# Four VectorE sums of a weight placed between the links of a routing chain, and a flag's transpose given another PSUM bank

## The chip, the cores and the metric

The kernel runs on one core of one Trainium2 chip. The metric is the device time of one execution in microseconds (us). Engines are named as in the profile: PE is TensorE's matmul and PEld its weight load, DVE is VectorE, ACT is ScalarE, POOL is GpSimd, and SP is SyncE, which here only issues transfers.

## What is computed

The reference is a causal attention with a window of 64 positions (8 batches, 8 heads, 576 positions, head size 64), whose output of 4608 rows by 512 is fed to a mixture of 8 experts. Each row goes to exactly one expert, and the choice depends on the row before it:

```python
fresh_e = int(np.argmax(logits[b, s]))
if s == 0 or local_gate[b, s] < 0.5:
    e = fresh_e
else:
    e = prev_e if prev_e >= 0 else fresh_e
prev_e = e
...
h = np.maximum(x[b, s] @ w1[e], 0.0)
out[b, s] = p[e] * (h @ w2[e])
```

So the expert of a row is either its own best expert or that of the row before. All is in float32; W1 is 512 by 1024 and W2 1024 by 512 for each expert.

## The kernel before

**Stages.** Attention runs first, for the first 135 us of the profiled execution or so. It writes its rows to a tensor in HBM (`xs`), the last of these writes from a tile `x` at 134.1 us. Then come blocks of rows, one expert each: two tiles of 128 rows are gathered from `xs`, turned on PE, multiplied by W1, put through a relu, multiplied by W2, scaled, and scattered to the output. Routing decides which rows make up a block. It is done in two parts: the rows of the first three of eight batches are routed during attention, which is enough to fill three blocks (numbered -1, -2 and -3), and all other rows are routed (`second`) while the blocks -1 and -2 run.

**The chain of routing.** `Router.gate` finds the expert of each row by scans on DVE over chunks of 128 rows, then over the chunks. Each step goes to PE to be transposed and back to DVE. In the profile's lines: DVE makes `vk`; PE turns it (L809); DVE copies it and scans twice (`loc` L814, `thru` L815); PE turns the last columns (L819, L820); DVE copies them and scans over the chunks (`crow` L822, `carry` L825); PE turns that (L829); DVE copies it and finishes the rows (`cbs` L831, `ex` L833); PE turns `ex` (L841); DVE copies it and compares (`et` L843, `oh` L845, a memset on `oh` L847); PE sums over rows (L853, L854); DVE copies the sums (L856), and some eighty small DVE instructions follow, which end in the tables `lo` and `hi` (L923, L924), and after the one-hot tables and the matmuls on them (L975), in the indices of the gathers.

PE's order is written out by hand: between two of the chain's transposes stand some matmuls of block -1's product with W1 (`hidden`, L1402). [...]

**The blocks' products.** The product with W2 (`big_result`, all matmuls at L1309) is done with seven products of half-size instead of eight. It needs four sums of quarters of W2, here called t1 to t4 (`right`, L1222, one DVE instruction of 128x1024 each, written to the tile `ws2`, shown as `ws`), and four sums of quarters of `h`, here called s1 to s4 (`halves`/`left`, L1214, 128x512 each, shown as `hs`). On PE the seven products stand in this order: one without sums, s1 with t1, s2 with t2, one without sums, s3 with t3, s4 with a quarter of W2, and a quarter of `h` with t4. (The code's lists count from zero: t1 is `t[0]`.) ACT copies some results out of PSUM (`keep`, L1314), and DVE combines others with what was kept (`put`, L1318, written to `y`). The last product adds on top of a bank from which the second `put` has read, and so waits for it.

**What sets the order on DVE.** In these stages a scheduler places DVE's instructions. A mark given to `issue_after` keeps an instruction behind the marked one. Before the change all four sums of W2, and the four of `h`, of block -1 stand behind `rt.link`, the memset at the end of the chain (L847); those of block -2 stand behind the making of `hi`. For block -1 that is done in `hidden`:

```python
if link and m == link[0]:
    mark = link[1]().ins
    with self.tc.issue_after(mark):
        self.prepare2(st)
```

**The flag.** `flag` turns a column on PE (L161) and reduces it on DVE, to tell whether a slow, rare path has to be taken. It stands after the last matmuls on the tables (L975), and `psum()` is routing's only bank, `r`, from which DVE copies the table (`t`, L977). A second pool, `ps_y` with two banks, is used only by blocks of fewer rows, which come later. Block -3's first stage stands behind the flag's last instruction.

**Transfers.** SP loads weights into a ring of four buffers, each load waiting for the buffer's last reader. POOL issues the gathers and the scatters, one after the other on its queue; a scatter waits until the one before it has landed.

Of the kernel before, what the change touches and what calls it, by code (L numbers as in the profile page):

```python
# [8 lines left out]
F32 = mybir.dt.float32  # L9
# [4 lines left out]
Alu = mybir.AluOpType  # L14
# [5 lines left out]
P = 128  # L20
B, H, S, DH = 8, 8, 576, 64
D = H * DH
E, F = 8, 1024
DK, FK = D // P, F // P
# [674 lines left out]
class Router:  # L699
# [9 lines left out]
    def __init__(self, ctx, tc, lt, xs, tabs, ident):  # L709
        self.nc, self.lt, self.xs, self.tabs, self.ident = tc.nc, lt, xs, tabs, ident  # L710
        self.pool = ctx.enter_context(tc.tile_pool(name="rt", bufs=1))
        self.tc, self.behind = tc, None
        self.rows_of(ctx, tc, "rt_oh1")

    def rows_of(self, ctx, tc, name, bufs=2):
# [47 lines left out]
    @staticmethod  # L763
    def last(ap):
        return ap.rearrange("p (c o) -> p c o", o=1)
# [5 lines left out]
    def gate(self, part, psum):  # L771
# [40 lines left out]
        loc = tl("loc", CMAX, P)[:n]  # L812
        thru = tl("thru", CMAX, P)[:n]
        vec.tensor_tensor_scan(loc, ts[:, 1, :], ts[:, 0, :], 0.0, Alu.mult, Alu.add)  # L814
        vec.tensor_tensor_scan(thru, ts[:, 1, :], self.zero[:n, :P], 1.0, Alu.mult, Alu.add)  # L815
        yield 1.5, True

        cps = psum()[:1, :2 * n].rearrange("o (i c) -> o i c", i=2)
# [3 lines left out]
        vec.tensor_copy(crow, cps)  # L822
        carry = tl("carry", 1, CMAX + 1)[:, :n + 1]
        vec.memset(carry[:, 0:1], 0.0)
        vec.tensor_tensor_scan(carry[:, 1:], crow[:, 1, :], crow[:, 0, :], 0.0, Alu.mult, Alu.add)  # L825
        yield 0.8, True

        cb = psum()[:n, :1]
# [1 line left out]
        cbs = tl("cbs", CMAX, 1)[:n]  # L830
        vec.tensor_copy(cbs, cb)  # L831
        ex = tl("ex", CMAX, P)[:n]
        vec.scalar_tensor_tensor(ex, thru, cbs, loc, Alu.mult, Alu.add)  # L833
        sm = by_chunk("sm")
        vec.tensor_reduce(sm, pa, axis=AX.X, op=Alu.add)
        vec.tensor_scalar(sm, sm, 1e-9, None, Alu.add)
# [7 lines left out]
        oh = self.oh[:, cs]  # L844
        vec.tensor_tensor(oh, last(et).to_broadcast(CE), self.io8.to_broadcast(CE), op=Alu.is_equal)  # L845

        self.link = vec.memset(oh[:CUT, 0, :] if part else oh[CUT:, n - 1, :], 0.0)  # L847
        yield 0.6, True


# [53 lines left out]
    def places(self, pl, n):  # L904

        vec = self.nc.vector

        def tl(name, p, n, dt=F32):
            return self.tl(name, p, CV, dt=dt)[:, :n]

        plc = tl("plc", P, n)
        vec.tensor_reduce(plc, pl, axis=AX.X, op=Alu.add)

        vec.memset(plc[CUT:, C1 - 1:C1], float(2 * N))
        if n > C1:
            vec.memset(plc[:CUT, C1:C1 + 1], float(2 * N))
        plc_i = tl("plc_i", P, n, dt=I32)
        vec.tensor_copy(plc_i, plc)
        lo_i = tl("lo_i", P, n, dt=I32)
        vec.tensor_scalar(lo_i, plc_i, P - 1, None, Alu.bitwise_and)  # L920
        vec.tensor_scalar(plc_i, plc_i, P.bit_length() - 1, None, Alu.arith_shift_right)
        lo, hi = tl("lo", P, n), tl("hi", P, n)
        vec.tensor_copy(lo, lo_i)  # L923
        self.link = vec.tensor_copy(hi, plc_i)  # L924
        return lo, hi

    def experts_of(self, ej, n, ends):
# [198 lines left out]
class Experts:  # L1126
# [87 lines left out]
            self.nc.vector.tensor_tensor(o, x, y, op=op)  # L1214
        return s1, s2, s3, s4

    def right(self, name, b):

        sub = Alu.subtract
        t1, t2, t3, t4 = self.sums(name, b)  # L1220
        for o, x, y in ((t1, b[0][1], b[0][0]), (t2, b[1][1], t1), (t3, b[1][1], b[0][1]), (t4, b[1][0], t2)):
            self.nc.vector.tensor_tensor(o, x, y, op=sub)  # L1222
        return t1, t2, t3, t4

    def sums(self, name, a):
        t = self.one.tile([P, 4, a[0][0].shape[1], a[0][0].shape[2]], F32, name=name)
        return [t[:, i] for i in range(4)]

    def prepare2(self, st):

        st["w2q"] = w2 = quarters(st["w2"], FK, D)
        st["w2t"] = self.right("ws2", w2)

    def halves(self, st):

# [150 lines left out]
    def hidden(self, st, quiet, step, link=None):  # L1386
        nc = self.nc
        if st["fast1"]:
            return self.big_hidden(st, step)
        if st["fast2"] and not link:  # L1390
            self.prepare2(st)
        n = BIG if st["big"] else st["rows"]
        st["h"] = h = self.wk.tile([P, FK, BIG], F32, name="h", bufs=1)
        each = min(512 // n, FK // 2)
        for g in range(FK // each):
            hp = self.ps_h.tile([P, each, n], F32, name="hp")
            for i in range(each):
                m = g * each + i
                for kk in range(DK):
                    for f in range(0, P, st["rows"]):  # L1400
                        a = slice(f, f + st["rows"])
                        nc.tensor.matmul(hp[a, i, :], lhsT=st["w1"][:, kk, m * P:(m + 1) * P][:, a],  # L1402
                                         rhs=st["xt"][:, kk, :n], start=(kk == 0), stop=(kk == DK - 1))
                if link and m == link[0]:
                    mark = link[1]().ins
                    with self.tc.issue_after(mark):
                        self.prepare2(st)
                if quiet and i + 1 < each:
                    step()
            o = h[:, g * each:(g + 1) * each, :n]  # L1410
            if (g % 2 or "half" in st) and not quiet:
                nc.vector.tensor_relu(o, hp)
            else:
                st["last"] = nc.scalar.activation(o, hp, Act.Relu)
            step()
        if st["fast2"]:
            st["hq"] = quarters(h, FK, BIG)
            with self.tc.issue_after(mark) if link else nullcontext():
                self.halves(st)

    def result(self, st, step, hooks=()):
# [41 lines left out]
    def run(self, ctx, rt, last=None):  # L1463

        tc = self.tc
        self.space(ctx)
        ps_r = ctx.enter_context(tc.tile_pool(name="ex_ps_r", bufs=1, space=PSUM))
        ctx.enter_context(tc.manual_schedule(engines={ET.PE, ET.SP}))
        rt.rows_of(ctx, tc, "rt_oh2", 3)
        jobs = self.jobs  # L1470

        def psum():
            return ps_r.tile([P, SC], F32, name="r")

        side = rt.second(psum)
        pause = 0.0

        def step():
            nonlocal side, pause
            pause, trip = max(pause - STEP, -1.5), False  # L1480
            while side and not trip and pause <= 0.0:
                w, trip = next(side, (0.0, None))
                pause += w + (0.6 if trip else 0.0)
                if trip is None:
                    side = None

        order = [-1 - n for n in range(FB)]
        between = [*range(NB, NB + SURE[1]), *range(KINDS[1] + 1, KINDS[1] + SURE[2])]
        quarters = list(range(KINDS[2], KINDS[2] + SURE[3]))
        for n in range(SURE[0]):  # L1490
            order.append(n)
            if n % 2 and between:
                order.append(between.pop(0))
            elif n % 4 == 2 and quarters:
                order.append(quarters.pop(0))
        order += between
        order.append(KINDS[1])
        assert not quarters
        jobs += [self.rows({}, n) for n in order[1:FB]]
        held = self.one.tile([1, 1], F32, name="held")  # L1500
        self.nc.sync.dma_start(out=held, in_=jobs[1]["x"][1][:1, :1])
        for i, n in enumerate(order[1:FB]):
            self.weights(jobs[1 + i], n)
        self.turn(jobs[0], True)
        step()
        pause += 3.4
        for i, n in enumerate(order):
            quiet = i < FB
            if i == FB - 1:
                while side:  # L1510
                    step()
                mark = last(psum()) if last else None

                ctx.enter_context(tc.manual_schedule(engines={ET.PE, ET.SP, ET.DVE, ET.Activation}))
                jobs.append(self.fetch(order[FB]))
                if jobs[i]["fast1"]:
                    self.prepare(jobs[i])
            if i + 2 > FB and i + 2 < len(order):
                jobs.append(self.fetch(order[i + 2]))
            if n >= KINDS[2]:  # L1520
                continue
            if i == 1:
                pause += 4.5
            with tc.issue_after(mark.ins) if i == FB - 1 and mark else nullcontext():
                self.hidden(jobs[i], quiet, step, ((FK - 1, lambda: rt.link), (FK - 3, lambda: rt.link))[i] if i < 2 else None)
            if i == 1:
                rt.behind = jobs[1]["last"]
            if i + 1 == len(order):
                self.result(jobs[i], step)
                continue  # L1530
            self.turn(jobs[i + 1], i + 1 < FB)
            if i + 2 < FB and jobs[i + 1]["fast1"]:
                self.prepare(jobs[i + 1])
            hooks = (step, ) * 6
            if order[i + 1] >= KINDS[2]:
                one, turned, two = self.quarter(jobs[i + 1])
                after = jobs[i + 2]
                hooks = one, turned, two, (lambda: None), (lambda: self.turn(after, False, True)), \
                    (lambda: self.prepare(after))
            self.result(jobs[i], step, hooks)  # L1540
# [63 lines left out]
```

## Time and profile before

| What | Value |
|---|---|
| median of three runs | 648.04 us |
| the three runs | 646.67, 648.04, 650.07 us |
| the profiled execution's own time | 645.2 us |
| its span, first to last instruction | 643.0 us |
| granted TensorE clock, mean | 0.997 |
| DVE, busy | 401.8 us (62%) |
| ACT, busy | 200.8 us (31%) |
| POOL, busy | 132.3 us (21%) |
| one of block -1's or -2's sums of W2 (DVE L1222 `ws<-w`), median | 1222 ns |

The span is 2.2 us shorter than the execution's own time; what lies around it is not in the trace. Times below are counted from the span's start. In the timeline a row is one instruction, or several alike merged, with its start, its length, and in brackets how long its engine sat idle before it and what ended that. In the list of waits a row names the waiting engine and line, what released it, the sum in us, the number of times and the longest.

### The profile page before, as it was taken

What the parts mean: (1) busy time and instruction counts of PE and PEld (TensorE: products, weight loads), DVE (VectorE), ACT (ScalarE), POOL (GpSimd) and SP (SyncE); (2) the same over time, 40 slices, a digit from 0 to 9 for tenths busy, and PEclk for the clock granted to TensorE, in tenths of its full rate; (3) what the DMA queues carried; (4) which work ended last, traced back from release to release, by engine and by line L of the source; (5) the groups of instructions that cost most, each with busy time, mean ns of one, the idle gap of its engine ahead of it and who ended that gap; (6) DMA issues with size and microseconds to landing.
All of it is one profiled execution on the core that took longest, in us unless ns stands there. A gap on an engine that the chain in (4) does not pass through costs nothing. (4 is left out here: it accounts for less than half of the span.)

```text
span 643.0 us, 14989 instructions
## 1 busy us (share of the span) xinstructions
PE 617.2 (96%) x6367; PEld 544.7 (85%) x6367; DVE 401.8 (62%) x752; ACT 200.8 (31%) x368; POOL 132.3 (21%) x132
## 2 busy tenths in 40 slices
PE   8898998898999999999999999999999999999995
PEld 7777776787889999978998999887997998899994
DVE  5776588858977865273553683363917752886730
ACT  2866765621572122112120312021211221213120
POOL 5422112320103202111302120221312022011101
PEclk9999999999999999999999999999999999999998
DMA  8989999979646655686957666769678556946501
GB/s 328 417 317 363 382 369 375 353 244 378 185 152 219 256 196 197 211 320 238 388 206 272 225 226 226 245 247 357 254 241 313 196 198 230 379 172 229 197 17 38
DMA packets 29318, 166.43 MB, mean 259 GB/s; under 512 B 8451, under 2 KB 9497, under 8 KB 20026
## 3 DMA queue, kind: packets, MB, share of 16 engines
q1 hardware_dynamic: 20394, 135.54, 58.2%
q0 software_dynamic: 8848, 29.85, 12.1%
q8 instruction: 52, 0.85, 0.5%
q14 instruction: 24, 0.20, 0.1%
HBM read 146.18 MB, written 19.59 MB: 258 GB/s over the span
## 5 line engine op out<-in xcount | busy, mean ns | idle before, releaser
L1382 POOL DMA_INDIRECT out_dram<-y,idx x36 | 41.3, 1147 | 344.5 <-DVE y L1318 198.2
L1309 PE MATMUL hp<-ws,hs 128*128 128x256 f32 x384 | 88.8, 380 | 1.9 <-DVE hs L1214 1.9
L1309 PEld LDWEIGHTS hp<-ws,hs 128*128 128x128 f32 x384 | 72.5, 190 | 12.8 <-DVE hs L1214 2.3
L1259 PE MATMUL hp<-xs,ws 128*128 128x128 f32 x672 | 79.6, 275 | 0.0
L1259 PEld LDWEIGHTS hp<-xs,ws 128*128 128x128 f32 x672 | 77.3, 192 | 0.0
L1318 DVE SCALAR_TENSOR_TENSOR y<-hp,xg,kept 128x256 f32<-128x256 f32 x48 | 22.6, 481 | 73.8 <-issue 47.0
L1402 PE MATMUL hp<-xt,w 128*64 128x64 f32 (+2 forms) x640 | 66.2, 276 | 0.0
L1402 PEld LDWEIGHTS hp<-xt,w 128*128 128x128 f32 (+1 forms) x640 | 60.8, 170 | 4.1 <-issue 0.7
L1309 PE MATMUL hp<-w,h 128*128 128x256 f32 x256 | 61.1, 382 | 0.0
L1270 DVE TENSOR_TENSOR h<-hp,keep 128x512 f32<-128x512 f32 x42 | 28.6, 690 | 48.7 <-PE hp L1259 48.7
L1157 POOL DMA_INDIRECT xg<-xs,gx x40 | 49.1, 1229 | 44.1 <-issue 38.1
L1259 PEld LDWEIGHTS hp<-xt,w 128*128 128x128 f32 x448 | 53.2, 192 | 2.7 <-issue 1.3
L1259 PE MATMUL hp<-xt,w 128*128 128x128 f32 x448 | 54.7, 275 | 0.0
L1309 PEld LDWEIGHTS hp<-w,h 128*128 128x128 f32 x256 | 47.2, 190 | 6.3 <-issue 0.4
L416 ACT ACTIVATE p<-sp 128x512 f32<-128x512 f32 x72 | 39.1, 595 | 37.2 <-PE sp L385 35.0
L431 PE MATMUL xo<-vb,p 128*64 128x74 f32 (+1 forms) x576 | 44.0, 228 | 6.8 <-issue 2.9
L421 DVE TENSOR_TENSOR p<-p,mask 128x1024 f32<-128x1024 f32 x29 | 36.3, 1252 | 19.6 <-ACT p L416 19.5
L385 PEld LDWEIGHTS sp<-w 64*64 64x64 f32 x1296 | 38.9, 138 | 11.2 <-issue 7.8
L431 PEld LDWEIGHTS xo<-vb,p 128*64 128x64 f32 x576 | 38.3, 136 | 10.3 <-issue 4.5
L385 PE MATMUL sp<-w 64*64 64x128 f32 (+1 forms) x1296 | 44.2, 270 | 1.6 <-ACT p L416 0.9
L1271 ACT ACTIVATE h<-h 128x512 f32<-128x512 f32 x42 | 26.3, 630 | 59.1 <-DVE h L1270 59.1
L431 PE MATMUL xo<-va,p 128*64 128x74 f32 (+1 forms) x576 | 44.1, 228 | 0.5 <-issue 0.5
(280 smaller groups left out, 955.9 us busy)
## 6 DMA issues: line engine op xcount, KB each, us to landing
w<-in_w_dram SPq DMA_DIRECT2D x42, 2048.0 KB, 8.9
w<-in_kq_dram SPq DMA_DIRECT2D x17, 1024.0 KB, 10.2
w<-in_w_dram SPq DMA_DIRECT2D x24, 512.0 KB, 9.3
xs<-x POOLq DMA_DIRECT2D x9, 1024.0 KB, 11.2
va<-in_v_dram SPq DMA_DIRECT2D x5, 1184.0 KB
vtt<-in_vt_dram SPq DMA_DIRECT2D x5, 1024.0 KB, 7.1
va<-in_v_dram SPq DMA_DIRECT2D x3, 1040.0 KB, 9.2
va<-in_v_dram SPq DMA_DIRECT2D x2, 520.0 KB, 7.1
```

The source lines that it names most:

```text
L385: nc.tensor.matmul(sp[j][c * WIN:(c + 1) * WIN, a:b], lhsT=kt[h, hp, block * WIN:(block + 1) * WIN], rhs=qt[h, hp, a:b], start=not biased, ...
L416: nc.scalar.activation(p[:, j], sp[j], Act.Exp, scale=DH ** -0.5)
L421: masked.append(nc.vector.tensor_tensor(p, p, m.to_broadcast([P, 2, SC]), op=Alu.mult))
L431: nc.tensor.matmul(xo[par * WIN:(par + 1) * WIN, j, s * VW:s * VW + n], lhsT=p[:, j, b * WIN:(b + 1) * WIN], rhs=w[:, s, 2 * hp + j, :n], ...
L1157: self.nc.gpsimd.indirect_dma_start(out=x, out_offset=None, in_=self.xs[:rows, :], in_offset=bass.IndirectOffsetOnAxis(ap=gx[:, s:s + 1], ...
L1259: nc.tensor.matmul(out[:, m, :], lhsT=a[:, kk, m * P:(m + 1) * P], rhs=b[:, kk, :], start=start and m + kk == 0, stop=stop and (m, kk) == ...
L1270: nc.vector.tensor_tensor(o, x, y, op=add)
L1271: nc.scalar.activation(o, x if y is None else o, Act.Relu)
L1309: nc.tensor.matmul(out, lhsT=a[:, m, :], rhs=b[:, m, :], start=start and m == 0, stop=stop and m == FK // 2 - 1, skip_group_check=True)
L1318: nc.vector.scalar_tensor_tensor(y[i][:, j * w:(j + 1) * w], x, pw[i], y2, Alu.mult, Alu.add)
L1382: self.nc.gpsimd.indirect_dma_start(out=self.out[:, :], out_offset=bass.IndirectOffsetOnAxis(ap=st["idx"][:, s:s + 1], axis=0), in_=y, in_ ...
L1402: nc.tensor.matmul(hp[a, i, :], lhsT=st["w1"][:, kk, m * P:(m + 1) * P][:, a], rhs=st["xt"][:, kk, :n], start=(kk == 0), stop=(kk == DK - 1))
```

## The change

The router keeps a list `links` of four instructions instead of one `link`: the second scan (`thru`), the scan over the chunks (`carry`), the step that finishes the rows (`ex`) and the memset on `oh`. `right` takes a mark for each of its four sums, so t1 is kept behind `thru`, t2 behind `carry`, t3 behind `ex`, and t4 behind the memset. The sums of `h` stay behind the last of the four. For block -2 all four marks are the making of `hi`, as before. The flag's column is turned into a bank of `ps_y`.

```diff
-        vec.tensor_tensor_scan(thru, ts[:, 1, :], self.zero[:n, :P], 1.0, Alu.mult, Alu.add)
+        self.links = [vec.tensor_tensor_scan(thru, ts[:, 1, :], self.zero[:n, :P], 1.0, Alu.mult, Alu.add)]
...
-        vec.tensor_tensor_scan(carry[:, 1:], crow[:, 1, :], crow[:, 0, :], 0.0, Alu.mult, Alu.add)
+        carried = vec.tensor_tensor_scan(carry[:, 1:], crow[:, 1, :], crow[:, 0, :], 0.0, Alu.mult, Alu.add)
+        self.links.append(carried)
...
-        vec.scalar_tensor_tensor(ex, thru, cbs, loc, Alu.mult, Alu.add)
+        self.links.append(vec.scalar_tensor_tensor(ex, thru, cbs, loc, Alu.mult, Alu.add))
...
-        self.link = vec.memset(oh[:CUT, 0, :] if part else oh[CUT:, n - 1, :], 0.0)
+        link = vec.memset(oh[:CUT, 0, :] if part else oh[CUT:, n - 1, :], 0.0)
+        self.links.append(link)
...
-        self.link = vec.tensor_copy(hi, plc_i)
+        self.links = [vec.tensor_copy(hi, plc_i)] * 4
...
-    def right(self, name, b):
+    def right(self, name, b, marks=()):
...
-        for o, x, y in ((t1, b[0][1], b[0][0]), (t2, b[1][1], t1), (t3, b[1][1], b[0][1]), (t4, b[1][0], t2)):
-            self.nc.vector.tensor_tensor(o, x, y, op=sub)
+        marks = [self.tc.issue_after(m) for m in marks] or [nullcontext() for _ in range(4)]
+        for o, x, y, mark in ((t1, b[0][1], b[0][0], marks[0]), (t2, b[1][1], t1, marks[1]),
+                              (t3, b[1][1], b[0][1], marks[2]), (t4, b[1][0], t2, marks[3])):
+            with mark:
+                self.nc.vector.tensor_tensor(o, x, y, op=sub)
...
-                    mark = link[1]().ins
-                    with self.tc.issue_after(mark):
-                        self.prepare2(st)
+                    marks = [x.ins for x in link[1]()]
+                    self.prepare2(st, marks)
...
-            with self.tc.issue_after(mark) if link else nullcontext():
+            with self.tc.issue_after(marks[-1]) if link else nullcontext():
                 self.halves(st)
...
-                mark = last(psum()) if last else None
+                mark = last(self.ps_y.tile([P, D], F32, name="yp")) if last else None
```

In the order of the changed program, DVE has t1 between L815 and L822, t2 between L825 and L831, t3 between L833 and L843, and t4 directly behind L847, followed by s3 and s1; only then come the copy of routing's sums (L856) and the rest of routing, with s2 and s4 among its first steps. The first two `put`s of block -1 stand a few small instructions later among them than before. PE, POOL and SP have the same instructions in the same order, but for the bank of the flag. On ACT, four of routing's one-hot rows (L967) move ahead of block -2's first relu (L1414).

More of the change, by code (lines that the diff above doesn't have):

```diff
@@ L711, in __init__ @@
         self.pool = ctx.enter_context(tc.tile_pool(name="rt", bufs=1))
-        self.tc, self.behind = tc, None
+        self.tc, self.behind, self.links = tc, None, []
         self.rows_of(ctx, tc, "rt_oh1")
@@ L1227, in sums, with prepare2 @@
         return [t[:, i] for i in range(4)]
-    def prepare2(self, st):
+    def prepare2(self, st, marks=()):
         st["w2q"] = w2 = quarters(st["w2"], FK, D)
-        st["w2t"] = self.right("ws2", w2)
+        st["w2t"] = self.right("ws2", w2, marks)
     def halves(self, st):
@@ L1524, in run @@
             with tc.issue_after(mark.ins) if i == FB - 1 and mark else nullcontext():
-                self.hidden(jobs[i], quiet, step, ((FK - 1, lambda: rt.link), (FK - 3, lambda: rt.link))[i] if i < 2 else None)
+                self.hidden(jobs[i], quiet, step, ((FK - 1, lambda: rt.links), (FK - 3, lambda: rt.links))[i] if i < 2 else None)
             if i == 1:
```

## The prediction

> **What bounds the kernel now.** The page's first part says which engine matters: PE is busy for 96% of the span. A change can therefore only gain where PE stands idle. I then read the list of PE's waits; these three of its rows touch the stages of the change:
>
> ```profile
> PE hp L1309 <- DVE hs L1214: 1.9, 1, 1.9
> PE hp L1309 <- DVE y L1318: 0.7, 1, 0.7
> PE r L161 <- DVE t L977: 0.4, 1, 0.4
> ```
>
> Together 3.0 us, each a single wait. The first is PE waiting for s1 with block -1's second product of W2, the second is the last product waiting for the second `put`, the third is the flag waiting for routing's bank. To place them I read the timelines of PE and DVE.
>
> ```profile
> 141.66 0.18 PE L819 MATMUL r<-ident,loc 23*1 23x23 f32 x1
> 143.72 0.18 PE L829 MATMUL r<-ident,carry 1*23 1x1 f32 x1
> ...
> 149.25 1.89 PE L1309 MATMUL hp<-w,h 128*128 128x256 f32 x8
> 153.06 3.72 PE L1309 MATMUL hp<-ws,hs 128*128 128x256 f32 x16 [1.92 <-DVE hs L1214]
> 156.62 1.89 PE L1309 MATMUL hp<-w,h 128*128 128x256 f32 x8
> ...
> 162.64 1.99 PE L1309 MATMUL hp<-ws,h 128*128 128x256 f32 x8 [0.67 <-DVE y L1318]
> ```
>
> ```profile
> 139.17 0.39 DVE L815 TENSOR_TENSOR_SCAN thru<-ts,zero 23x128 f32<-23x128 f32 x1
> 141.91 0.19 DVE L822 COPY crow<-r 1x46 f32<-1x46 f32 x1 [2.36 <-PE r L820]
> 142.14 0.20 DVE L825 TENSOR_TENSOR_SCAN carry<-crow 1x23 f32<-1x23 f32 x1
> 143.94 0.14 DVE L831 COPY cbs<-r 23x1 f32<-23x1 f32 x1 [1.60 <-PE r L829]
> 144.12 0.34 DVE L833 SCALAR_TENSOR_TENSOR ex<-thru,cbs,loc 23x128 f32<-23x128 f32 x1
> 146.03 0.18 DVE L843 COPY et<-r 128x23 f32<-128x23 f32 x1 [1.57 <-PE r L841]
> ...
> 146.66 0.07 DVE L847 MEMSET oh<- 64x8 f32 x1
> 147.10 2.36 DVE L1222 TENSOR_TENSOR ws<-w 128x1024 f32<-128x1024 f32 x2 [0.38 <-DMA w<-in_w_dram]
> ```
>
> DVE stands idle for 2.36, 1.60 and 1.57 us inside the chain, and right behind it has four sums of W2 and four of `h` to do, mixed with routing. Those are what PE waits for from 151.1 on.
>
> [...] The trace has 1222 as the median; in a row the starts lie 1.14 apart, and I use that. [...] all rows above stand in program order; so a late t1 holds up the chain, and then PE. [...] t1 will overlap the last two gathers, issued from 138.8 to 141.0; no run here shows such a pair yet, and I price it at 0. Those gathers feed block -3, needed some 50 us later.
>
> **Part 1: do the sums fit?** t1 can begin when `thru` ends (139.56), if its inputs are there. W2's four loads were issued from 119.8 to 122.5 and the slowest took 12.9, so it was in by 135.4. But t1 also waits for the last write of `xs`, whose tile lay where `ws` lies:
>
> ```profile
> L533 POOL DMA_DIRECT2D xs<-x x1: 796/796/796, 134.1 to 134.1; - x1
> ...
> DMA to landing us min/median/max: 4.6/4.6/4.6
> ```
>
> So that landed at 138.7, 0.9 before `thru` ended. The instruction has ten waits; the 0.38 of idleness before it at 147.10 is, I take it, their cost, since the load named there was long done. t1 runs 139.94 to 141.16, and `crow` waits for PE until 141.91 anyway: hidden, with 0.75 to spare. t2 runs from 142.34 (end of `carry`) plus some 0.1 for two waits to 143.66; `cbs` starts at 143.94. t3 runs from 144.46 to 145.68; `et` starts at 146.03. Cost 0, spare 0.3 each. Without that cover PE itself has slack: `carry` ends at 142.34 and L829 runs at 143.72, so 1.3 us of lateness cost nothing.
>
> **Part 2: what DVE gains.** Before, the four sums begin at 147.10. After, only t4 follows the memset, at 146.73. DVE saves three sums (3 x 1.14 = 3.42) and 0.37 of waits, less 0.13 in which s1 waits for block -1's last relu (ACT L1414, 147.95 + 0.60 = 148.55). It is 3.66 earlier wherever the same instructions lie behind it.
>
> **Part 3: the first wait.** t4 146.73, s3 147.87, s1 at about 148.6, done at 149.3. PE wants s1 at 149.25 + 8 x 0.216 = 150.98. s2, behind the copy L856 (0.45), ends by 150.3; PE wants it at 152.7. s4 ends at 151.1; wanted at 157.9. The wait is gone. PE reaches the second product at 150.98 instead of 153.06; with 0.1 for the slower first matmul after a stop, that is 2.19.
>
> **Part 4: the second wait.** From 150.98 PE has five products of 8 x 0.216 = 1.73 before the last: it wants the last at 159.62. The second `put` starts at 162.11 before. After, it stands further back. Before, the scan `qend` ends its turn at 161.44; taking out the first `put` (0.39), the 3.66, and adding back 0.13 of latency which that `put` used to fill gives 157.51. Then the first `put` (0.39) and nine of routing's instructions, three of 0.38 and six of 0.07 to 0.08 (1.58): the second `put` starts at 159.48 and, as it takes 0.47, ends at 159.95. PE followed 0.06 behind it before (162.58, 162.64), so it starts at 160.01. PE waits 0.39 instead of 0.84 between starts; 162.64 - 160.01 = 2.63 gained up to here. The first `put`, at 157.5, finds its product done at 156.3.
>
> **Part 5: block -2.** ACT has four one-hot rows (0.30 each) before the first relu. They wait for `lo` at 168.84 - 3.66 = 165.2, end at 166.4, and the relu, ready at 168.17 - 2.63 = 165.5, is late by 0.9. PE wants that bank for the fourth group, at 164.47 - 2.63 + 48 x 0.216 = 172.2. Cost 0.
>
> **Part 6: the flag.** In another bank, L161 needn't wait: 0.36. But what is late next is a gather. Block -2's first scatter is issued at 191.59, behind a `put` that PE releases; it lands 8.3 later, POOL's next scatter goes out at 200.64 and the gathers at 201.92 and 203.22; the second lands at 206.85, and PE's second group of transposes starts at 206.99 instead of at 206.68. That chain moves by 2.63, as its first link does. PE comes 2.99 earlier, and waits 0.36 longer. I count the flag as 0, with 0.36 as the other end.
>
> Sum: 2.19 + 0.44 + 0 = 2.63. After 207 PE has no wait above 0.25 us till 635.5, so the gain reaches the end. Profiled execution 645.2 - 2.6 = 642.6. The median of the runs is 2.8 above that execution; the same gain there gives 648.04 - 2.6 = 645.4.
>
> **The rivals.** *A, as above*: 645.4; 2.2 to 3.0 by the spares, 645.0 to 645.8. *B, more is kept*: the second `put` comes in time (0.39) and the gather chain is quicker, so that the flag's 0.36 stays: 3.4, 644.6. For it: with the loads 2.6 earlier, the 8.3 us of that scatter may shrink; against: that load, released by PE at 190.75, moves along with it. *C, nothing arrives*: the gathers at 203.22 don't move, for the scatter is tied to the traffic rather than to PE, and PE stands till 206.99 as before: 648.0. Against it: every transfer in that stretch is released by PE. *D, slower*: t1 is held by the last write of `xs`, DVE with it, and PE at L829. For t1 to harm, it must end after 143.2 (then `crow` and `carry`, 0.43, and 0.06 to PE), so the write must land after 141.6. From there PE loses one for one; at 144.3, 10.2 after its issue, the gain is gone, and at 147.5, 13.4 after, the kernel is 3.2 slower, 651.3. Over all nine such writes the trace has:
>
> ```profile
> DMA to landing us min/median/max: 4.6/11.2/14.4
> ```
>
> So the usual landing would do it. Against: the other eight ran beside loads. This one had W2's tail only until 135.4, and SP issues the next loads at 143.2, behind a gather. That holds in every run of this program.
>
> **How the numbers follow.** The half-percent bound, about what a measurement of this kernel can tell from no change, is 3.24 us. A has 0.58; by the runs' spread (1.7 to either side of the middle) some four tenths of it, 0.22, show over 0.5%. B has 0.22, of it 0.18 over. C has 0.11, all within. D has 0.09: 0.07 slower, 0.02 within. Faster 0.40, within 0.53, slower 0.07. Range: from B's 644.6 less the spread of 1.7 (642.9) to C's 648.0 and a third of the spread (648.6); outside lie most of D and the edges of the others.
>
> **What would show it.** Right: the L1222 rows start at about 139.9, 142.4, 144.5 and 146.7; `crow` is still released by PE; no wait of PE on `hs` or at L161, one of 0.2 to 0.4 on `y`; block -2's L1402 at 161.8 instead of 164.47; a wait of 0.6 to 0.8 at PE's L1190 near 204. Wrong: DVE idle before the first L1222 on a DMA of `xs`, and PE idle before L829, which is D; or PE idle elsewhere after 165 by as much as was won.

## The result, and the profile after

Over 22 runs of each kernel on one chip the median went from 647.49 to 644.32 us: a ratio of 0.9952 with a 95% interval of 0.9931 to 0.9972, that is 3.1 us less (1.8 to 4.5). The forecast was 2.6 us less. The profiled execution took 643.61 us, 1.6 less than that of before.

That execution's attention part was 1.83 us longer than in before's (block -1's first matmul with W1 starts at 134.44 instead of 132.61), and what follows PE's last matmul was 0.9 shorter. Both scatter without any edit: in a repeat of the kernel before, shown below, the same matmul starts at 136.81, and in a second profile of the changed kernel the end takes 7.4 us instead of the first one's 6.7. So I compare *PE's stretch*: from that matmul to the end of PE's last one. It went from 502.87 to 500.38, 2.49 less. "Relative" times below count from the same matmul.

The list of PE's waits in the profile after has these two rows of the stages concerned:

```profile
PE tp L1192 <- DMA xg<-xs,gx: 0.4, 1, 0.4
PE hp L1314 <- DVE y L1323: 0.4, 1, 0.4
```

The wait for `hs` and the flag's are gone; the one on `y` is down from 0.7 to 0.4; and a new one stands at block -3's transposes. (Lines have moved: L1309 is now L1314, L1222 is L1227, L1214 is L1216, L1190 is L1192.) The timeline of DVE shows why the first has gone:

```profile
140.99 0.39 DVE L815 TENSOR_TENSOR_SCAN thru<-ts,zero 23x128 f32<-23x128 f32 x1
141.30 1.19 DVE L1227 TENSOR_TENSOR ws<-w 128x1024 f32<-128x1024 f32 x1
143.74 0.19 DVE L822 COPY crow<-r 1x46 f32<-1x46 f32 x1 [1.25 <-PE r L820]
...
144.09 1.19 DVE L1227 TENSOR_TENSOR ws<-w,ws 128x1024 f32<-128x1024 f32 x1
145.76 0.14 DVE L832 COPY cbs<-r 23x1 f32<-23x1 f32 x1 [0.49 <-PE r L830]
...
146.21 1.20 DVE L1227 TENSOR_TENSOR ws<-w 128x1024 f32<-128x1024 f32 x1
147.85 0.18 DVE L844 COPY et<-r 128x23 f32<-128x23 f32 x1 [0.44 <-PE r L842]
148.47 1.21 DVE L1227 TENSOR_TENSOR ws<-w,ws 128x1024 f32<-128x1024 f32 x1
```

The first three sums fit into idle places of the chain, and the fourth follows it. `crow`, `cbs` and `et` still wait for PE, by 1.25, 0.49 and 0.44 us instead of 2.36, 1.60 and 1.57; so no sum holds the chain. The timeline of PE:

```profile
151.07 1.89 PE L1314 MATMUL hp<-w,h 128*128 128x256 f32 x8
152.80 3.62 PE L1314 MATMUL hp<-ws,hs 128*128 128x256 f32 x16
...
161.96 1.99 PE L1314 MATMUL hp<-ws,h 128*128 128x256 f32 x8 [0.36 <-DVE y L1323]
```

The second product follows the first without a stop. Relative to the stretch's start, three places tell where the gain comes and stays: block -1's last product is 2.51 earlier (30.03 to 27.52), the flag 3.03 (61.01 to 57.98), block -3's second group of transposes 2.51 (74.37 to 71.86). What the flag gained over the last product is gone again at the transposes.

### The profile page after: what moved, and what is told of

Its sections match the earlier page's. It is cut to its first block, busy times and chain, and to the rows that moved or that the text cites. A ratio compares the mean times of both kernels' runs of the same rounds, so it can differ in the third digit from the quotient of the medians.

```text
span 641.5 us, 14988 instructions
## 1 busy us (share of the span) xinstructions
PE 616.2 (96%) x6367; PEld 543.7 (85%) x6367; DVE 401.2 (63%) x752; ACT 200.9 (31%) x368; POOL 130.0 (20%) x132
## 5 line engine op out<-in xcount | busy, mean ns | idle before, releaser
L1314 PE MATMUL hp<-ws,hs 128*128 128x256 f32 x384 | 88.7, 380 | 0.0
L1314 PEld LDWEIGHTS hp<-ws,hs 128*128 128x128 f32 x384 | 72.6, 190 | 10.5 <-issue 0.8
L1314 PE MATMUL hp<-w,h 128*128 128x256 f32 x256 | 61.1, 382 | 0.0
L1314 PEld LDWEIGHTS hp<-w,h 128*128 128x128 f32 x256 | 47.2, 190 | 6.3 <-issue 0.4
```

Source lines behind the costliest of these rows:

```text
L1314: nc.tensor.matmul(out, lhsT=a[:, m, :], rhs=b[:, m, :], start=start and m == 0, stop=stop and m == FK // 2 - 1, skip_group_check=True)
```

## The experiments

Most kernels have one profiled execution each and are compared by PE's stretch; three were timed over several executions.

### The flag alone

```diff
 # the kernel before
-                mark = last(psum()) if last else None
+                mark = last(self.ps_y.tile([P, D], F32, name="yp")) if last else None
```

> The kernel before with the flag in the second pool's bank, nothing else changed. Measure: PE's stretch, from the start of block -1's first matmul with W1 to the end of PE's last matmul (502.87 before, 500.38 after), which leaves out attention's part. Theory (the flag's 0.36 is taken back by the gather): 502.9, no wait at L161, and PE's wait for the gather before its transposes grows from 0.31 to about 0.7. Rival (the flag counts by itself): 502.5.

Measured: 644.47 us, stretch 503.42, later than either theory. The flag's own wait was gone, but at another place something else had happened. In this run's table of windows (from and to, length, then busy us and instructions of PE, PEld, DVE, ACT and POOL, the granted clock, DMA's share, GB/s):

```profile
150.00:152.00 2.00, 0.38 (x2) 0.00 (x0) 2.00 (x4) 0.47 (x1) 0.00 (x0) 1.00 1.02 391
152.00:154.00 2.00, 1.70 (x6) 1.40 (x7) 2.00 (x5) 0.00 (x0) 0.00 (x0) 0.75 1.03 420
154.00:156.00 2.00, 2.00 (x6) 1.64 (x5) 2.00 (x11) 0.47 (x1) 0.00 (x0) 0.50 1.02 412
```

and the same stage of the kernel before, in its profiled execution:

```profile
151.00:153.00 2.00, 0.14 (x1) 0.00 (x0) 2.00 (x5) 0.47 (x1) 0.00 (x0) 1.00 1.02 399
153.00:155.00 2.00, 1.94 (x9) 1.73 (x10) 2.00 (x6) 0.00 (x0) 0.00 (x0) 1.00 1.03 420
```

Both show PE idle for `hs`; behind that wait the kernel before ran at full clock, and this run at half (0.50) for 3.4 us. In the 2 us from 154 PE did 6 matmuls, where the 0.216 us each that before's matmuls take undisturbed (eight in 1.73) makes 9. Its timeline has the price:

```profile
152.30 5.41 PE L1309 MATMUL hp<-ws,hs 128*128 128x256 f32 x16 [1.92 <-DVE hs L1214]
```

5.41 us for the two products, where before took 3.72. As the wait on `y` vanished behind it, 1.05 was left at block -1's last product (relative 31.08 instead of 30.03). So the stretch can't be set against before's first profile. It can be set against the repeat of before, shown below, which has the same half clock and the same 31.08 at the last product: there the flag's edit puts PE ahead by 0.53 at the flag (61.55 instead of 62.08), by 0.35 at block -3's second group of transposes, and by 0.47 at relative 400. In this pair, where PE comes a microsecond later than in the first profile, most of the flag's gain is kept. The run also raised a new question: does the wait cost more than its length?

### The links alone

```diff
 # the changed kernel
-                mark = last(self.ps_y.tile([P, D], F32, name="yp")) if last else None
+                mark = last(psum()) if last else None
```

> The kernel after with the flag back in routing's bank: only the sums are moved. Theory: PE's stretch 500.4, as with the whole change; a wait of 0.36 at L161 and none or 0.1 to 0.2 for the gather. Rival (the flag counts by itself): 500.7 to 500.8.

Measured: 646.1 us, stretch 500.55, and PE waits 0.36 at L161 again. That is 0.17 longer than with the flag's edit: PE is 0.50 later at the flag, and a third of that reaches the end. A second profile of the changed kernel, below, came out 0.16 longer than this run, because it waited longer for the gathers; so 0.17 isn't clear of that scatter. The gain is in the links.

### Where the sums may stand

First, all four marks set to `thru`; then the four in two pairs.

```diff
-        marks = [self.tc.issue_after(m) for m in marks] or [nullcontext() for _ in range(4)]
+        marks = [self.tc.issue_after(marks[0]) for _ in marks] or [nullcontext() for _ in range(4)]
```

> The kernel after with all four marks on the first link, thru: three sums come before crow and the fourth before carry. Theory (past a slack of 1.3 us whatever holds up DVE ahead of a link holds up PE, one for one): carry ends at about 145.0 instead of 142.3 on the clock of the kernel before, PE idles some 1.3 us before the transpose of carry, stretch 501.3 to 501.8. Rival (all that counts is that the sums are out of the way early): 500.0 to 500.4.

```diff
-        marks = [self.tc.issue_after(m) for m in marks] or [nullcontext() for _ in range(4)]
+        marks = [self.tc.issue_after(marks[i // 2]) for i in range(len(marks))] or [nullcontext() for _ in range(4)]
```

> The kernel after with t1 and t2 behind thru, t3 and t4 behind carry. Theory (each link has 1.2 to 1.4 us of slack on PE): PE doesn't idle in the chain though crow is copied 0.4 late and cbs 1.1 late; DVE is up to 1.1 earlier afterwards, so the wait for the second put (0.36 after) shrinks to 0 to 0.1: stretch 500.0 to 500.1. Rival (a late link is a late PE at once): PE idles 0.4 to 1.1 in the chain, stretch 500.8 to 501.5.

With all four behind `thru` DVE did three of them before `crow` and one before `carry`, and the chain's PE step waited:

```profile
145.66 0.16 PE L830 MATMUL r<-ident,carry 1*23 1x1 f32 x1 [0.66 <-DVE carry L825]
```

Stretch 500.96 (644.06 us): between the theories, as 0.66 was idle where I had 1.3. The direction is the theory's, that sums past the slack are paid for by PE. The slack is what I had put: `carry` ended 1.98 later than in the changed kernel (relative 11.70 instead of 9.72) and PE's step behind it came 0.73 later, so 1.25 was free. The delay was smaller than I had put, in part since the first sum began 0.31 behind `thru`'s start and not 0.77. Two and two: stretch 500.11 (641.54 us), as expected; no idle PE in the chain, and no wait on `y`. So the four places of the change aren't the best ones: two are enough.

### The kernel before once more

> The kernel before once more, for how well PE's stretch repeats. Theory (what differs from run to run is attention's part, which ends when loads allow): stretch 502.7 to 503.1 where the clock isn't throttled, with waits of 1.9, 0.7 and 0.4 again, while the start of the stretch moves by up to 2 us. Rival (the stretch itself scatters as the whole run does): off by over 1 us, and then the differences of 0.3 us between the experiments mean nothing.

No edit. Measured: 652.11 us, stretch 505.86, a miss; its start, too, moved by 4.2 us and not by 2. Two things stood in it that before's first profile doesn't have: half clock from 158.1 to 161.5, right behind the wait for `hs` (1.93), with the same 31.08 at the last product as in the flag's run; and 2.0 us more behind relative 400. Compared matmul by matmul, 1.66 of these are lost at relative 412, where small matmuls stood three times with no releaser shown, and 0.3 near 499. Four kernels were run side by side here: this one, the one with the gathers ahead, and the two with five copies. Each lost 1.94 to 1.98 us behind relative 400, at the same matmuls; none of the other ten profiles did. The cause stays open, and these four are compared only up to relative 400.

### The scatter behind the gathers

```diff
 # the changed kernel; block -2's second scatter is issued behind the four gathers
-            self.nc.gpsimd.indirect_dma_start(
+            self.got = self.nc.gpsimd.indirect_dma_start(
...
+        if defer:
+            return lambda: self.scatter(st, 1, y[1])
...
+                with tc.issue_after(self.got.ins):
+                    later()
```

> The kernel after with block -2's second scatter moved behind the four gathers on POOL's queue. Theory (the wait of 0.43 at the transposes comes from that scatter, which waits for the one before it to land): the gathers go out some 8 us sooner, no wait at the transposes, and the flag's 0.36 is kept: stretch 499.6 to 499.8 instead of 500.38. Rival (the gathers are late for their own tables or for traffic): the wait stays, 500.3 to 500.4.

Measured: 644.6 us; block -3's second group of transposes at relative 71.02 instead of 71.86, with no wait, and at relative 400 PE is 0.94 ahead of the changed kernel. The stretch, 501.41, has the disturbance just named (without it, 499.4 where 499.6 to 499.8 was expected). POOL's timeline in the changed kernel:

```profile
190.90 0.98 POOL L1387 DMA_INDIRECT out_dram<-y,idx  x1 [17.48 <-DVE y L1323]
200.19 0.98 POOL L1387 DMA_INDIRECT out_dram<-y,idx  x1 [8.31 <-issue]
201.48 1.00 POOL L1159 DMA_INDIRECT xg<-xs,gx  x1 [0.30 <-issue]
```

The second scatter stands 8.31 us on POOL until the first has landed, and the gathers stand behind it. That is what took the flag's gain back; with the gathers ahead they start 4.43 us behind the first scatter's start (194.87 and 190.44 in that run) instead of 10.58.

### The last write of `xs` made late

Copies on POOL ahead of that write hold it back (five take 5.5 us); five of 128x1024 in the kernel before, five in the changed kernel, ten in the changed kernel. In the changed ones `crow` is also kept behind t1, so that the scheduler can't let it pass.

```diff
+LATE = 5
...
+            held = None
+            for n in range(LATE if sc == NSC - 1 else 0):
+                junk = pp.tile([P, 2, SC], F32, name="p")
+                held = nc.gpsimd.tensor_copy(junk.rearrange("p i x -> p (i x)"),
+                                             x[:, 2:].rearrange("p c h j d -> p (c h j d)"))
+            with tc.issue_after(held.ins) if held else nullcontext():
+                nc.gpsimd.dma_start(
...
```

> The kernel before with five copies of 128x1024 on POOL put ahead of attention's last write of xs (they copy from the tile that is written, and nothing reads the copies), so that it is issued some 5 us later. Theory: block -1's sums start at 147.1 on the clock of before, after the write has landed at about 144; no loss, stretch 502.7 to 503.2.

> The same five copies in the kernel after, with t1 still kept ahead of crow. Theory (t1 waits for that write, DVE for t1, PE for carry): t1 starts when the write has landed, at about 144 on the clock of before, DVE stands idle until then, PE idles 1.5 to 3 us before the transpose of carry, and most or all of the gain is gone: stretch 501.7 to 503.2. Rival (t1 needs only W2): t1 starts behind thru as before, no wait, 500.3 to 500.6.

Measured: 650.45 and 649.78 us, stretches 508.75 and 504.80, both above what was expected. In the first, 2.9 of the 5.9 us more than before are lost in the chain, 1.0 to half clock behind the wait for `hs`, and 1.9 to the disturbance. In the second, DVE did wait before t1. The trace names no releaser, but the write, issued at 142.49, would land at about 147.1 by the 4.6 us that it took in before:

```profile
147.32 1.23 DVE L1234 TENSOR_TENSOR ws<-w 128x1024 f32<-128x1024 f32 x1 [1.85 <-issue]
```

but PE didn't wait for `carry`, where I had expected 1.5 to 3 us. Two things: 1.85 fits into the slack behind t1 (the next run gives it as 2.1), and the copies themselves held the chain, by 2.8 of idle PE at `vk`'s transpose in both kernels alike. DVE's timeline with the copies:

```profile
136.06 1.18 DVE L798 TENSOR_TENSOR pa<-lt,mx 128x184 f32<-128x184 f32 x1
...
138.26 1.01 DVE L807 SCALAR_TENSOR_TENSOR fresh<-lt,begin 128x23 f32<-128x23 f32 x1
```

and in the kernel before without them:

```profile
135.13 0.34 DVE L791 TENSOR_TENSOR pa<-lt,mx 128x184 f32<-128x184 f32 x1
...
136.01 0.18 DVE L800 SCALAR_TENSOR_TENSOR fresh<-lt,begin 128x23 f32<-128x23 f32 x1
```

So the delay had to be longer. With ten copies:

> The changed kernel with its last write of xs made later still, by ten copies on POOL ahead of it (five were in the run before this one), and crow kept behind t1. What is computed is the same. Rival D's mechanism (t1 waits for that write and holds the chain): the write is issued at about 148 to 154 and lands 152 to 158, t1 starts within 0.3 us of its landing, VectorE is idle for 5 to 11 us before it, and PE is idle for 5 to 11 us before the transpose of carry; PE's stretch, 504.8 with five copies, becomes 510 to 516, later than the kernel before's 508.75 with five copies. If t1 did not depend on it: t1 right behind thru, and the stretch within 1.5 us of 504.8.

Measured: 659.5 us, stretch 515.09. POOL issued the write at 152.02, it landed at 156.59, and DVE's timeline has t1 right behind it:

```profile
143.50 0.40 DVE L822 TENSOR_TENSOR_SCAN thru<-ts,zero 23x128 f32<-23x128 f32 x1
156.67 1.23 DVE L1234 TENSOR_TENSOR ws<-w 128x1024 f32<-128x1024 f32 x1 [12.77 <-issue]
```

The first row of PE's list of waits in that run:

```profile
PE r L837 <- DVE carry L832: 10.6, 1, 10.6
```

t1 begins 0.08 behind the landing, and `crow`, next in DVE's order, at 157.81, though the transposes on PE that it reads had run at 145.61 and 145.64. So rival D's mechanism is real: t1 is tied to that write, and the chain and PE to t1. (The clock halved behind this wait too, from 151.8 to 162.0.) Of DVE's 12.77 PE lost 10.63; about 2.1 is the slack behind t1. (DVE's own wait came out longer than the 5 to 11 I had put.) In the kernel as it is the write was issued at 135.92 and landed at 140.49, 0.9 before `thru` ended, and nothing of it is paid.

### The wait filled with matmuls that nobody needs

The theory put to the test: the wait for `hs` (1.92 us) costs its length and then, by the half clock behind it (3.4 us in the flag's run), some more; a PE kept busy during the wait would lose only the length.

```diff
 # the kernel before, on PE between block -1's first and second product with W2
+FILL = 7
...
+        if self.jobs and st is self.jobs[0]:
+            busy = self.ps_y.tile([P, D], F32, name="yp")[:, :P]
+            for _ in range(FILL):
+                nc.tensor.matmul(busy, lhsT=self.ident, rhs=self.ident, start=True, stop=True)
```

> The kernel before, with seven products of ident by ident (128x128) placed on PE between block -1's first and second product of W2, into a bank of ps_y that nobody reads. Their results are not used, so the kernel computes what it did. They fill about 1.5 of the 1.92 us in which PE waits for s1 there; the operands of the next products come no earlier. Theory (the wait itself costs 1.92 and, in most executions, a stretch of 3.4 us at half of TensorE's clock behind it, about 1.05 us at the last product): no stretch at half clock behind this place, the wait for s1 shown as 0.2 to 0.6 us, and over many runs the kernel 0.5 to 1.0 us faster than before (ratio 0.9985 to 0.9992) although not one useful instruction moved. Rival (the halved clock has another cause, such as the load of the hs products or chance): half clock still there from the first hs product on, and a ratio of 1.000 or a little above.

> The changed kernel once more, beside the filled one. Theory: ratio 0.995 (3.2 us), of which 2.5 are the two waits and some 0.7 the clock; so it should be ahead of the filled kernel by about 2.3 to 2.6 us. No half clock within 10 us behind the first hs product. Rival (all of it is the waits): 2.5 us, and the filled kernel at 1.000. PE's stretch from block -1's first product with W1 to the end of its last product: 500.4 where the later part is undisturbed.

The changed kernel is run once more beside it, unedited. Measured:

| Kernel | runs | median, us | ratio to before | 95% interval | mean granted clock |
|---|---|---|---|---|---|
| before | 35 | 647.92 | | | 0.9943 |
| before, wait filled | 22 | 647.15 | 0.9988 | 0.9971 to 1.0006 | 0.9964 |
| changed | 13 | 643.74 | 0.9931 | 0.9910 to 0.9951 | 0.9965 |

In the filled kernel's profile the matmuls take 1.72 us and the wait for `hs` is down to 0.36; in its table of windows the clock stays whole:

```profile
154.00:156.00 2.00, 1.83 (x16) 1.62 (x14) 2.00 (x4) 0.47 (x1) 0.00 (x0) 1.00 0.99 354
156.00:158.00 2.00, 1.80 (x8) 1.62 (x9) 2.00 (x6) 0.00 (x0) 0.00 (x0) 1.00 1.03 414
```

Its last product is at relative 30.02, exactly where before's undisturbed profile has it (30.03): filling wins nothing of the wait. That it keeps the clock, one profile can't show, as before's first profile kept it too; the mean clock of the runs can: without the wait, or with it filled, it is higher by 0.0021 (standard error 0.0006). That is 0.0021 x 645 = 1.35 us of clock, or 0.8 (standard error 0.2) of a stretch of 3.41 us at half (1.71). In the first set the changed kernel's 22 executions had only 0.9955, and before's clocks aren't on record there, so the size is less sure than this error says. Of the profiles, three of the four with the unfilled wait (the flag's, the repeat of before, the one with five copies; not before's first) had the half clock behind it, and none of the changed kernel's family had it at that product. The time agrees in size (0.8 us less, expected 0.5 to 1.0), but its interval holds zero, so the time alone doesn't show it.

The changed kernel gained 4.5 us here (3.2 to 5.8), more than the 3.2 expected, and 3.4 over the filled one where I expected 2.3 to 2.6. The two intervals of its ratio overlap; I can't say whether more than the clock and the two waits stands in this second set. Its profiled execution has a stretch of 500.71 where 500.4 was expected: it waited 0.77 for the gathers at block -3's transposes, and the first profile 0.43.

### A better version

Two sums behind `thru` and two behind `carry`, and the gathers ahead of the scatter: the edits of two runs above together.

> The changed kernel with two edits: two sums behind thru and two behind carry (none behind the later links), and block -2's second scatter put behind the four gathers that followed it on POOL. From the single looks: the first edit takes away the wait on y (0.36 of PE), the second the wait at the transposes of block -3 (0.84). So PE's stretch is 499.2 to 499.6 where it was 500.4, and the time 0.8 to 1.2 us below the changed kernel's; ratio to the kernel before 0.9930 to 0.9940. Rival (what is won there is taken back at the next late transfer, as the flag's 0.36 was): the same ratio as the changed kernel, 0.995, with a new wait of PE between block -3's transposes and its first relus.

Measured over 7 runs: median 642.83 us, ratio to before 0.9913 (0.9881 to 0.9944); the changed kernel beside it had 0.9931, so the median is 0.9 us below that one's (0.8 to 1.2 was expected). PE's stretch is 499.20 instead of 500.38. It has no wait on `y`, none at L161 and none at block -3's transposes; its POOL timeline:

```profile
188.91 0.98 POOL L1389 DMA_INDIRECT out_dram<-y,idx  x1 [17.91 <-DVE y L1323]
193.35 1.00 POOL L1159 DMA_INDIRECT xg<-xs,gx  x1 [3.45 <-DVE gx L988]
...
199.96 1.02 POOL L1389 DMA_INDIRECT out_dram<-y,idx  x1 [0.30 <-issue]
```

The gathers now wait only for their indices. The last product is 0.30 earlier than in the changed kernel, the second group of transposes 1.13, and PE's end 1.18: nothing is taken back. By the traces this is the best kernel of the study; its time interval overlaps the changed kernel's.

## Why the prediction was right, and what was mis-sized

**Part 1, the places.** Right. Counted from `thru`'s start, t2, t3 and t4 were due 3.23, 5.29 and 7.56 us later and came after 3.10, 5.22 and 7.48. t1 began 0.31 behind `thru`'s start, where I had 0.77: the 0.38 for its ten waits wasn't paid again. The traces list these waits as instructions of DVE's sequencer (DVEq; durations in ns, then the first and the last start in us). In the kernel before and in the changed one:

```profile
L1222 DVEq EVENT_SEMAPHORE  x6: 21/50/50, 146.6 to 147.1; - x6
L1227 DVEq EVENT_SEMAPHORE  x5: 21/50/50, 140.6 to 141.0; - x5
```

In the kernel before, the five ahead of t1 (the sixth belongs to the next sum) start from 146.64 to 147.00, beside a memset of only 0.07, and DVE stands for 0.38. In the changed kernel five such instructions start from 140.60 to 140.96, while DVE is busy with the scan `loc` (140.59 to 141.06), and nothing is lost. t1 also ran beside two gathers, issued at 140.61 and 141.87, and took 1.19 us, where 1.22 was the median before; the price of 0 for that, my estimate, was right.

**Part 2, DVE's lead.** Right: the first sum of `h` was due 8.70 behind `thru`'s start and came after 8.61.

**Parts 3 and 4, the two waits.** In the profile right for the first: 2.19 was forecast, and the second product started 2.09 earlier and the third 2.19, as the forecast had it with 0.1 for the slower first matmul after a stop (the 16 matmuls behind the wait took 3.72 in before, and 3.62 without it in the changed kernel). The second gave 0.32 where 0.44 was forecast (the last product moved by 2.51): the second `put` started 20.43 behind `thru`'s start and not 20.31. A wait on `y` of 0.36 stayed (0.2 to 0.4 forecast).

**Part 5, ACT.** Right at 0: no wait of PE on ACT in block -2.

**Part 6, the flag.** Right at about 0 for the changed kernel: 0.52 ahead at the flag, gone at the transposes. Its cause, the scatter ahead of the gathers on POOL, is shown by moving it. It isn't 0 everywhere: 0.17 was kept in the pair with the links, and 0.47 in the pair without them at half clock. What is kept depends on how late PE comes for the gathers.

**The sum and the time.** 2.63 was forecast for the profiled execution and PE's stretch fell by 2.49. Over the runs it was 3.1 in one set and 4.5 in the other, against 2.6. The step that was mis-sized is the one that carried the profile's sum over to the median: "the same gain there". Part 3 priced the wait for `hs` at its own length, as the one profiled execution showed it. In two other profiles with that wait (the flag's, the repeat of before) 3.4 us at half clock stood behind it, and the last product came 1.05 us later. With 0.8 of a stretch in the mean, as the mean clocks have it, my estimate of the sum is 2.5 + 0.8 x 1.05 = 3.3; with half a stretch, as the grid described at the end would have it by chance, 3.0. The first measurement, 3.1, lies between these two; the second, 4.5, lies above both, though its interval begins at 3.2. The change, -0.48% and -0.69%, lies at the bound of half a per cent, on both sides of it.

**The rivals.** B's time (644.6) was closer to the measured 644.32 than A's 645.4, but not by its mechanism: in the changed kernel the flag's gain was not kept. C fell: counted from the stretch's start, the scatter went out 2.52 earlier and the first gather behind it 2.27. D has its mechanism, but not in this program: the write landed as early as its 4.6 us said.

## What to carry to other kernels

Here a wait of the bottleneck engine cost more than its length: behind 1.92 us of idle PE three of four profiles had half clock, and in two of them 3.4 us of it made the last product 1.05 us later. So price what the matmuls behind such a wait lose, too, over several executions and not only the profiled one. The idle places between the links of the chain through PE (2.36, 1.60 and 1.57 us) were free for work up to their own length and the time by which PE would come later anyway, here 1.25 us: two sums behind `thru` cost nothing, and three with a fourth behind `crow` cost PE 0.7. Two places were as good as four. When an early gain vanishes, read the queue of the engine that issues the next transfer: here a scatter stood for 8.31 us in front of four gathers that didn't need it.

## What was unexpected in the hardware

**The half clock came on a grid, and mostly behind windows with 1.85 us of idleness or more.** In each trace's clock records the stretches at half clock start whole multiples of 3.413 us apart, to within 0.01: in the repeat of before at 103.5, 158.1 and 646.2, which are 16 and then 143 such steps. I cut all fourteen traces into windows on that grid, from some 20 to 600 us, and summed PE's idle time in each. Of the 9 windows with 1.85 us or more, 8 were followed by half clock; of the 10 with 1.72 to 1.85, 3; of the 2346 with less, 1. The bounds of these groups were chosen to fit the counts. In the profiled execution of the kernel before, a boundary at 151.6 cut the wait into 0.46 and 1.48, and nothing followed. In the repeat of before a window a little more than half idle, 1.93 of 3.41 us, was followed by half clock. That the phase of the grid is chance would make a 1.92-us wait trip in about half of the executions (an estimate from the step of 3.413 and the bound of 1.85); 3 of 4 were seen, too few to tell.

**Some of DVE's small operations took longer beside copies on POOL.** Beside them `pa` took 1.18 us instead of 0.34 and `fresh` 1.01 instead of 0.18; in the run with ten copies `pa` fell between two of them and took 0.34 again.
